# A hand-written instruction order: its first third and its identity products replaced

## The chip, the core and the metric

One core of a Trainium2 chip. The metric is the time of one launch in microseconds, the median of the runs on the device; lower is better. The kernel before has 238.1 us as the median of three runs (237.83 to 238.64).

## What is computed

An attention with blocks sorted by a Sinkhorn matrix, then a feed-forward network with a PReLU between its two products. Batch 4, 8 heads, 768 positions in 8 blocks of 96, head width 64; the network has 3072 tokens, width 512 and 2048 hidden units.

```python
for _ in range(5):                      # Sinkhorn: P is 4 x 8 x 8 x 8
    P = np.exp(P - np.max(P, axis=-1, keepdims=True))
    P = P / (np.sum(P, axis=-1, keepdims=True) + 1e-09)
    P = P / (np.sum(P, axis=-2, keepdims=True) + 1e-09)
k_sorted = np.einsum('bhij,bhjcd->bhicd', P, k_b)
v_sorted = np.einsum('bhij,bhjcd->bhicd', P, v_b)
scores = scale * np.matmul(q_b, k_sb.transpose(0, 1, 2, 4, 3))
attn = softmax(scores)                  # rows of one block of 96
out = np.matmul(attn, v_sb)
h = x @ w_in                            # x: attention output, heads side by side
y = (np.maximum(h, 0.0) + alpha * np.minimum(h, 0.0)) @ w_out
```

## The kernel before

**Work.** Attention is cut into 32 groups: group g is block g % 8 of batch g // 8, with all 8 heads. For each group there are: `s1`, the scores (8 products, L712 for batches 1 to 3, L715 for batch 0); the row maximum on VectorE (L721); the exp on ScalarE; `o`, the product with sorted v (L768); reciprocal and scaling on VectorE (L776, L779); and a turn of the result into xT, by TensorE and a copy in batches 0 and 1 (L794, L800) and by a transposing DMA later (L787). Batch 0 uses another way to the exp: the scores are made a second time, transposed, and the maximum is subtracted by products with the identity (L736 and L727, called `s2` here), so that one exp (L759) gives what `o` reads. In the other batches the exp (L748) is turned by a transposing DMA (L753).

**Preparation.** q, k and v are loaded by GpSimd's queue, which casts to bf16. For batch 0 `prep_q` turns q on TensorE (L600) and ScalarE copies the result out; for batches 1 to 3 a transposing DMA on SyncE's queue, `turn_q` (L409), does it. `prep_k` and `prep_v` (L629 and L669; L600 and L674 in batch 0) multiply k and v by a matrix that holds the Sinkhorn weights, 6 and 8 steps for each batch, each followed by a copy out of PSUM (0.6 to 0.7 us, L372) on ScalarE or VectorE. Before that, `conv_k` and `conv_v` (L616, L653, L658) spread the loaded k and v in SBUF, fp32 words copied on GpSimd or VectorE. The Sinkhorn rounds alternate between VectorE (L515 to L532) and one exp on ScalarE per round (L521). `spread0` and `spread` (L539, L557, L560) bring the result to all partitions; the matrix BDK is made on VectorE (L543).

**The network.** `ffn1(ga, gb, ft)` makes one tile of 128 hidden units for the tokens of groups ga to gb (4 products, L823), of 192 tokens for groups 0 to 3 and of 384 later; ScalarE takes the negative part (L833) and VectorE combines (L836). `ffn2(t)` makes 128 tokens of the result in four parts of 4 products (L863), then a copy (L372) and a store on SyncE's queue (L877). `w_in` and `w_out` come in four and two loads on GpSimd's queue (L908, L913).

**Order.** No scheduler runs when the kernel is built. Each operation is added to a graph with its reads and writes, and with a duration in nanoseconds; `arrange` (L158) then puts the operations on their engines in the order of the table `SEQ` (L36), whose numbers are the operations in the order in which they were added (a letter names the engine where there is a choice: p GpSimd, a ScalarE, d VectorE). Each engine, and each DMA queue, works strictly in that order. `emit` (L205) sets semaphore waits from the reads and writes. Neither reads the durations. `WARM` (L32) lists identity products: `89:14:y` puts 14 products of 128 x 512 with the identity before operation 89 on TensorE, into a PSUM bank whose content nobody reads (L808); four more are an operation of their own (L965).

Operations that the text speaks of: 44, 51, 58, 65, 72 the exps of the Sinkhorn rounds; 79 `spread0`; 81 to 92 `prep_q` and its copies; 93 to 105 `prep_k` of batch 0; 114 to 129 `prep_v` of batch 0; 149 and 158 `s1` of groups 0 and 1, 150 and 159 their maxima; 151 and 160 their `s2`; 134 and 135 the two loads of w_out; 273 to 276 `ffn2(0)`; 178 to 183 `turn_q` of batch 1; 402 and 403 the loads of v, 404 that of k for batch 2; 411 to 418 the loads of q for batch 2; 419 `s1` of group 8, 420 its maximum; 519 the `ffn1` tile at which the common order of TensorE begins.

## Time and profile before

| | |
|---|---|
| median of 3 runs | 238.1 us |
| span of the profiled execution, first to last instruction | 236.6 us |
| around the span (median less span) | 1.5 us |
| TensorE busy | 229.2 us (97%) |
| VectorE, ScalarE, GpSimd busy | 169.8, 151.6, 73.0 us |
| DMA moved | 31.36 MB |

The profile is of one execution, and its own time outside the span isn't recorded; the median less the span stands for it. Busy time of TensorE holds the identity products, and ends of products are modelled, so the distance from the start of one group of products to the start of the next is the better measure of what a group takes. In a timeline row stand start, length, engine, line, operation, tiles, and in brackets the idle time of the engine before it and what ended it. "PEld" is the weight load of TensorE. "DMA share" in the windows can be over 1, since packets overlap.

### The profile page before, as it was taken

Reading aid. Unit: us, or ns where it says so; the run is one execution under the profiler, and the core shown is the slowest. Engines: PE = TensorE matmul, PEld = TensorE weight load, DVE = VectorE, ACT = ScalarE, POOL = GpSimd, SP = SyncE. Lnnn points to the kernel's source line nnn. Section 1 sums busy time; section 2 is a strip of 40 time slices with the busy share of each in tenths; the row PEclk is TensorE's granted clock in tenths of the full one; section 3 lists DMA queues with packets and bytes.
Section 4 is the critical chain, followed back from the end, with each engine's and each line's share of the span. In section 5 each row is a group of like instructions: output and inputs, shape, how many; then the busy total and the mean of one; then the engine's idle time right before and its main releaser. Section 6 shows DMA issues by size and latency. Waiting matters only on the chain.

```text
span 236.6 us, 6266 instructions
## 1 busy us (share of the span) xinstructions
PE 229.2 (97%) x2532; PEld 142.2 (60%) x2532; DVE 169.8 (72%) x354; ACT 151.6 (64%) x423; POOL 73.0 (31%) x139
## 2 busy tenths in 40 slices
PE   7998998999999999999999999999999999999995
PEld 3446676687666666556566665655555555555543
DVE  4748796989899997868887667676766587744350
ACT  4475265587887988886678786756864646453332
POOL 7958812915659620338590020000000000000000
PEclk9999999999999999999999999999999999999999
DMA  5999999999989999899998796542642323400033
GB/s 96 212 213 168 211 217 202 179 209 158 191 88 167 152 120 173 119 210 166 165 111 114 188 164 135 98 90 52 125 92 82 97 50 79 140 0 1 0 133 135
DMA packets 71453, 31.36 MB, mean 133 GB/s; under 512 B 64504, under 2 KB 65280, under 8 KB 71424
## 3 DMA queue, kind: packets, MB, share of 16 engines
q0 software_dynamic: 22896, 13.63, 42.0%
q1 hardware_dynamic: 48528, 17.33, 37.8%
q8 instruction: 20, 0.33, 0.5%
q14 instruction: 9, 0.07, 0.1%
HBM read 27.28 MB, written 6.29 MB: 142 GB/s over the span
## 4 chain that ended last, share of the span: by engine, by line
PE 76%; DMA 17%; POOL 6%; issue 1%; ACT 0%; POOLq 0%
PE psH L823 31%; PE psYP L863 28%; DMA w_out_bf<-in_moe_w_out_dram 10%; PE psS L863 3%; PE psS L712 3%; DMA VST<-in_v_dram 3%; PE psO L768 3%; PE psYP L669 2%; DMA ET<-Esb 2%; PE psYP L629 1%; DMA QTz<-QN 1%; POOL w_in_bf L908 1%; PE psO L863 1%; PE psS L727 1%; POOL VDz L456 1%; PE psO L794 1%
## 5 line engine op out<-in xcount | busy, mean ns | idle before, releaser
L836 DVE SCALAR_TENSOR_TENSOR hT<-t,omaT,psH 128x384 bf16<-128x384 f32 (+1 forms) x139 | 77.4, 571 | 36.6 <-ACT t L833 35.1
L823 PE MATMUL psH<-xT,w_in_bf 128*128 128x384 bf16 (+1 forms) x556 | 96.9, 311 | 0.0
L833 ACT ACTIVATE t<-psH 128x384 f32<-128x384 f32 (+1 forms) x139 | 63.1, 461 | 50.3 <-PE psH L823 49.2
L863 PE MATMUL psYP<-w_out_bf,hT 128*128 128x512 bf16 x336 | 83.2, 379 | 1.3 <-DMA w_out_bf<-in_moe_w_out_dram 1.3
L823 PEld LDWEIGHTS psH<-xT,w_in_bf 128*128 128x128 bf16 x556 | 49.5, 98 | 28.9 <-DVE hT L836 1.6
L863 PEld LDWEIGHTS psYP<-w_out_bf,hT 128*128 128x128 bf16 x336 | 30.8, 98 | 30.1 <-DMA w_out_bf<-in_moe_w_out_dram 1.8
L748 ACT ACTIVATE Esb<-psS,nf 96x96 bf16<-96x96 f32 x192 | 46.1, 345 | 2.0 <-DVE nf L721 2.0
L721 DVE TENSOR_REDUCE nf<-psS 96x8 f32<-96x768 f32 x24 | 22.8, 951 | 6.4 <-PE psS L712 6.0
L658 POOL COPY VDz<-VST 64x192 f32<-64x192 f32 x39 | 20.4, 524 | 20.3 <-DMA VST<-in_v_dram 16.6
L779 DVE TENSOR_TENSOR xq<-psO,rec 96x512 bf16<-96x512 f32 x31 | 21.2, 683 | 0.5
L401 POOL DMA_DIRECT2D QN<-in_q_dram x24 | 19.8, 833 | 3.3 <-DMA QTz<-QN 2.7
L616 POOL COPY KSz<-KS 64x256 f32<-64x256 f32 x28 | 11.1, 397 | 31.6 <-PE psYP L629 19.8
L712 PEld LDWEIGHTS psS<-KT,QTz 128*96 128x96 bf16 x192 | 12.1, 124 | 3.3 <-DMA QTz<-QN 0.2
L768 PEld LDWEIGHTS psO<-VS,ET 112*128 112x128 bf16 x248 | 11.1, 98 | 3.6 <-ACT ET L759 0.2
L808 PE MATMUL psYP<-identb 128*128 128x512 bf16 x40 | 12.8, 453 | 0.4 <-ACT identb L372 0.4
L372 ACT ACTIVATE VS<-psYP 112x512 bf16<-112x512 f32 x15 | 10.3, 687 | 4.2 <-PE psYP L669 2.2
L768 PE MATMUL psO<-VS,ET 112*128 112x65 bf16 x248 | 12.7, 194 | 0.0
L712 PE MATMUL psS<-KT,QTz 128*96 128x96 bf16 x192 | 12.6, 208 | 0.0
L372 ACT ACTIVATE KT<-psYP 128x512 bf16<-128x512 f32 x15 | 9.0, 599 | 2.8 <-PE psYP L629 1.8
L669 PEld LDWEIGHTS psYP<-BDV,VDz 128*128 128x128 bf16 x192 | 8.2, 98 | 2.7 <-POOL VDz L658 0.4
L372 ACT ACTIVATE outstg<-psYP 128x512 f32<-128x512 f32 x13 | 7.7, 604 | 3.2 <-PE psYP L863 3.2
L669 PE MATMUL psYP<-BDV,VDz 128*128 128x64 bf16 x192 | 9.5, 193 | 0.2 <-POOL VDz L658 0.2
(137 smaller groups left out, 198.8 us busy)
## 6 DMA issues: line engine op xcount, KB each, us to landing
out_dram<-outstg SPq DMA_DIRECT2D x23, 256.0 KB, 2.5
KS<-in_k_dram POOLq DMA_DIRECT2D x3, 768.0 KB, 13.3
QN<-in_q_dram POOLq DMA_DIRECT2D x24, 96.0 KB, 4.4
w_in_bf<-in_moe_w_in_dram POOLq DMA_DIRECT2D x4, 512.0 KB, 17.3
w_out_bf<-in_moe_w_out_dram POOLq DMA_DIRECT2D x2, 1024.0 KB, 23.9
VST<-in_v_dram POOLq DMA_DIRECT2D x4, 384.0 KB, 17.6
hT<-in_q_dram POOLq DMA_DIRECT2D x1, 768.0 KB, 7.6
VST<-in_v_dram POOLq DMA_DIRECT2D x1, 768.0 KB, 11.1
```

The source lines that it names most:

```text
L372: return e.activation(o, i, ACTF.Copy) if e is nc.scalar else e.tensor_copy(o, i)
L658: G.add(SHIFT, lambda e, o2=o2, i2=i2: e.tensor_copy(o2, i2), {"dve": 424, "pool": 525}, r=vst, w=[("VDz", u % VSL, th)], prio=prio)
L669: inst = e.matmul(AP(t, off + dd * 64, [[row, 128], [1, 64]]), AP(VDz, (u % VSL * 4 + dd // 2) * 256 + dd % 2, [[VSL * 1024, 128], [2, 128]]),
L712: inst = e.matmul(o, AP(QTz[n], hp * 3072 + h4 * 768 + i * 96, [[6144, 128], [1, 96]]), AP(KT[n], (h4 * 8 + i) * bk, [[ld, 128], [64, 2], ...
L721: G.add(DVE, lambda e: e.tensor_reduce(AP(nx, 0, [[8, 96], [4, 2], [1, 4]]), AP(psX, 0, [[1024, 96], [512, 2], [96, 4], [1, 96]]), AxisLis ...
L748: inst = e.activation(AP(Esb[me], p * 128, [[1024, 96], [64, 2], [1, 48]]), AP(psX, (p // 4) * 512 + (p % 4) * 96, [[1024, 96], [48, 2], [ ...
L768: inst = e.matmul(AP(psZ, hp * 512 + h4 * 68, [[1024, 128], [1, 65]]), AP(ET[me] if far else ET[m], pos(h4, hp) * 96, [[800, nk], [1, 128] ...
L779: G.add(DVE, lambda e: e.tensor_tensor(out=AP(xq[me], 0, [[512, 96], [256, 2], [64, 4], [1, 64]]), in0=AP(psZ, 0, [[1024, 96], [512, 2], [ ...
L823: inst = e.matmul(AP(pt, poff, [[1024, 128], [1, n]]), AP(w_in_bf, kt * DFF + ft // 2 * 256 + ft % 2, [[KT_TILES * DFF, 128], [2, 128]]), ...
L833: G.add(ACT, lambda e: e.activation(AP(t1[tb], 0, [[384, 128], [1, n]]), AP(pt, poff, [[1024, 128], [1, n]]), ACTF.Relu, scale=-1.0), t_ac ...
L836: G.add(DVE, lambda e: e.scalar_tensor_tensor(out=AP(hT, ft * RING + tok % RING, [[FT_TILES * RING, 128], [1, n]]), in0=AP(t1[tb], 0, [[38 ...
L863: inst = e.matmul(AP(bank[0], bank[1], [[1024, 128], [1, n]]), AP(hT, ft * RING + tok % RING, [[FT_TILES * RING, 128], [1, 128]]), AP(w_ou ...
```

## The change

`SEQ` and `WARM` are replaced, and the durations given to `G.add`. The operations, their reads and writes, the buffers and the loads are the same 1227. TensorE's order differs in its first 145 operations and is the same in the last 254; SyncE's order differs in the first 14 of 85; on GpSimd the last 42 operations, on ScalarE the last 156 and on VectorE the last 189 are in the same order, and what stands ahead of them differs. 47 operations change engine (copies out of PSUM between ScalarE and VectorE; `conv_k` and `conv_v` between GpSimd and VectorE; on balance GpSimd has nine operations fewer, VectorE seven more, ScalarE two more). The identity products of the list go from 43 to 30. Some places, counted from 1 on the engine named:

| operation | before | after |
|---|---|---|
| loads of k and v, batch 0 (5, 6), GpSimd | 6, 8 | 3, 4 |
| first load of w_in (130), load of k, batch 1 (138), GpSimd | 13, 10 | 6, 12 |
| exp of Sinkhorn round 5 (72), ScalarE | 10 | 7 |
| maxima of groups 1 and 0 (159, 150), VectorE | 52, 56 | 50, 51 |
| `s2` of group 2 (186), TensorE | 37 | 35 |
| `ffn2(0)`, first part (273), TensorE | 49 | 61 |
| `s1` of group 8 (419), TensorE | 100 | 106 |
| loads of v for batch 2 (403, 402), GpSimd | 49, 62 | 61, 65 |

```diff
@@ -30,56 +30,57 @@
 WARM = """
-89:14:y 79:8:y 93:2:y 104:2:y 158:6:y 118:1:y 128:4:y 162:1:y 153:3:h 205:1:y 207:1:y
+83:15:y 79:2:y 100:2:y 158:7:y 160:1:y 136:1:y 156:2:i
 """
 
 SEQ = """
-0 7 11 2 3 1 4 8 9 22 42 28 14 43 44 45 46 19 47 18 5 48 49 50 15 51 39 52 53 6 54 55 25 56 138 57 58 23 29 59 12p
-60 61 130 62 63 64 31 65 32 66 37 13 67 68 89 69 83 81 70 84 71 87 131 10 91 88 85 132 72 40 73 90 74 133 75 86 76
-41 77 82 134 78 79 92 26 80 147 93 148 102 94d 103a 104 95 105a 100 98 96a 99a 97d 109d 106p 35 111d 112d 108p 34
-16 101a 36 38 33 107p 158 149 114 115d 146 110p 118 250p 159 116 248p 119a 120 113p 121d 124 30 117d 160 135 125a
-249p 254p 24 136 161 122 137 144 150 126 127a 143 123d 145 128 151 129d 253p 247d 20 17 152 162 21 163 164 141 153
-177 154 140 155 165 156 142 166d 184 157a 167 185 196 193 168 186 169 194 197 195 199 198 187 202 170 27 203 205
-200 204 188 201 214 206 220 215 217 189 218 207 221 219 222 226 216 229 190 227 223 230 273 228 224 171 208 231 225
-235 191 236 238 192a 237 232 239 261 251 262 209 313p 233 252a 240 210 263 347p 211 139 255 241 270 234 212 403 264
-256a 213d 291 404 301d 271 242 175 259 292 258p 274 260a 257p 272 265 352p 267 243 266 279 244 311p 293 280 268
-300p 281 282 269 312p 294 245 174 304d 285 310p 246d 275 286 351p 283 287 284 338 348p 302 339 295 305p 303a 314
-288 296 315 306 289 316 340 307a 290 176 297 320 341 317 276 318 178 321 319 298 322 379 299a 308 380 323 179 309a
-342 326 324 343 349 344 327 381 350a 325 328 345 353 382 346d 329 354d 332 330 383 333 331 357 277a 334 180 335
-572p 384 361 385 336 402 373 362 337 360p 358a 183 363 419 359d 574p 386 364 420 391p 367 365 374 355p 368 366 421
...
+0 7 2 17 10 3 1 4 8 9 5 42 11 6 43 44 14 45 46 47 48 130 49 50 51 32 52 23 53 54 22 55 26 56 25 57 28 138 58 37
+40 16 59 33 13 60 61 62 63 64 65 24 83 66 19 81 67 21 87 68 91 131 69 85 70 89 71 132 72 39 73 74 29 133 82 75
+76 38 77 20 78 88 12p 79 92 134 80 86 35 100 84 147 93 102 94a 98 95 101a 99d 104 90 105d 96a 103a 97p 158 107d
+113p 149 106d 116 108d 110p 18 159 118 114 111p 119a 150 15 160 117a 115a 109d 124 34 112p 122 125a 120 123d 161
+136 121d 128 126 129d 151 127a 137 162 152 177 163 164 36 248p 153 165 148 154 184 155 166a 250p 185 135 156 167
+157a 146 186 168 169 143 170 196 187 193 247d 139 253d 199 194 205 200 195 144 197 188 201 202 198 249p 206 214
+142 217 215 254d 203 41 207 218 204 216 220 189 171 208 219 223 190 226 221 224 238 222 227 191 225 229 192a 228
+232 239 209 233 235 230 210 236 234 240 231 237 264 211 241 251 261 252d 258p 212 262 291 140 265 175 263 255
+273 266 256a 257p 292 145 259 270 213d 174 293 141 260d 271 272 242 301p 294 282 172 243 304d 267 244 279 312p
+268 338 351d 305p 245 269 274 313p 300d 246a 339 280 404 283 295 302 281 310p 340 303a 284 352p 296 297 288 348p
+341 285 298 347p 306 286 299d 289 379 287 311p 307a 342 290 314 380 308 315 317 309a 275 176 343 318 27 316 319
+349 320 344 276 321 350d 323 322 353 356d 324 326 354d 359p 381 355p 325 277d 357 31 382 329 178 358d 345 373
+330 327 360d 346a 328 179 331 383 388 384 332 390d 389a 395p 335 385 374 180 333 391p 336 334 30 337 392 403 361
...
@@ -375,16 +376,16 @@
...
-        op = G.add(PE, f, t_pe(*[(n, 128)] * 4), r=[("xT", g % 16) for g in range(ga, gb)] + [("w_in", ft // 8 * 2 + x) for x in range(2)],
+        op = G.add(PE, f, {192: 330, 384: 650}[n], r=[("xT", g % 16) for g in range(ga, gb)] + [("w_in", ft // 8 * 2 + x) for x in range(2)],
...
```

The other hunks change durations alone, as the last one shown does.

More of the change, by code (lines that the diff above doesn't have):

```diff
@@ L514, in dv @@
         def dv(fn, r, w):
-            G.add(DVE, fn, 210, r=r, w=w, prio=pr)
+            G.add(DVE, fn, 191 if w[0] in ("rs", "cs") and w == r else 255 if w == ["cs"] else 208, r=r, w=w, prio=pr)
         for it in range(5):
@@ L562, in f @@
             return inst
-        G.add(PE, f, 100 * rows, r=["Pb", "selk"] + [("xT", 1)] * late, w=PSP, prio=prio)
+        G.add(PE, f, 130 * n + 110, r=["Pb", "selk"] + [("xT", 1)] * late, w=PSP, prio=prio)
         for y, mk in ((0, "mkj"), (1, "mkjV"))[:1 + late]:
@@ L607, in prep_q @@
         t, off, row, keys = bank
-        G.add(PE, pairs(hT, 8192, u, identb, 0, 128, bank), 372, r=[("QS", 0), "identb"], w=keys, prio=prio)
+        G.add(PE, pairs(hT, 8192, u, identb, 0, 128, bank), 254, r=[("QS", 0), "identb"], w=keys, prio=prio)
         o = AP(QTz[0], 8 * u, [[6144, 128], [96, 32], [48, 2], [1, 8]])
         i = AP(t, off, [[row, 128], [2, 32], [1, 2], [64, 8]])
-        G.add(ACT, lambda e: copy(e, o, i), t_act(512), r=keys, w=[("Q0", u)], prio=prio)
+        G.add(ACT, lambda e: copy(e, o, i), 569, r=keys, w=[("Q0", u)], prio=prio)
     def conv_k(b, u, prio):
@@ L633, in prep_k @@
         if b:
-            G.add(PE, f, 250, r=[("KSz", u % 3, hp) for hp in range(2)] + [("BDM", b)], w=keys, prio=prio)
+            G.add(PE, f, 232, r=[("KSz", u % 3, hp) for hp in range(2)] + [("BDM", b)], w=keys, prio=prio)
         else:
-            G.add(PE, pairs(KS[n], 0, u, BDK, 0, 512, bank), 372, r=ks + [("BDK", 0)], w=keys, prio=prio)
+            G.add(PE, pairs(KS[n], 0, u, BDK, 0, 512, bank), 254, r=ks + [("BDK", 0)], w=keys, prio=prio)
         ld, bk = 4 * NB * BK0, BK0
@@ L678, in prep_v @@
         if b:
-            G.add(PE, f, 250, r=[("VDz", u % VSL, th) for th in range(2)] + [("BDV", b)], w=keys, prio=prio)
+            G.add(PE, f, 232, r=[("VDz", u % VSL, th) for th in range(2)] + [("BDV", b)], w=keys, prio=prio)
         else:
-            G.add(PE, f, 374, r=[("VD", u), "VD0", ("BDK", 0)], w=keys, prio=prio)
+            G.add(PE, f, 277, r=[("VD", u), "VD0", ("BDK", 0)], w=keys, prio=prio)
         o = AP(VS[n], 8 * u, [[64 * 65, 112], [65, 64], [1, 8]])
         i = AP(t, off, [[row, 112], [1, 64], [64, 8]])
-        G.add(EITHER, lambda e: copy(e, o, i), {"act": 685, "dve": 690}, r=keys + [("VS1", n)], w=[("VS", n, u)],
+        G.add(EITHER, lambda e: copy(e, o, i), {"act": 687, "dve": 690}, r=keys + [("VS1", n)], w=[("VS", n, u)],
               prio=prio)
@@ L890, in burst @@
         return inst
[L891 removed]
+    G.add(PE, burst, 1240, r=["bz"], w=["psSw", "psS0", "psS1"], prio=-120)
     load_q(0, -98)
@@ L964, in bass_sinkhorn_attn__then__act_prelu_kernel @@
             spread([1, 2, 3], 1)
-            G.add(PE, lambda e: warm(e, 4, (psH, 0)), 300, r=["identb"], w=[("psH", 0, 0), ("psH", 0, 1)], prio=1)
+            G.add(PE, lambda e: warm(e, 4, (psH, 0)), 864, r=["identb"], w=[("psH", 0, 0), ("psH", 0, 1)], prio=1)
         if b + 1 < B:
```

180 lines of the change are left out of this document (90 added, 90 removed).

## The prediction

> **What bounds the kernel now.** I read the page first, then the busy time by stages, then the timeline of each engine through the first 80 us, then the rows of single lines. The page says that TensorE is the bound:
>
> ```profile
> span 236.6 us, 6266 instructions
> PE 229.2 (97%) x2532; PEld 142.2 (60%) x2532; DVE 169.8 (72%) x354; ACT 151.6 (64%) x423; POOL 73.0 (31%) x139
> DMA  5999999999989999899998796542642323400033
> ```
>
> But 97% holds the identity products that only fill waits, and matmul ends are modelled. The windows, cut at the first FFN1 product, at the stop for w_out, at the first score product of batch 1 (s1 of group 8) and where the two orders of TensorE become the same, tell more (busy us, granted clock, DMA share, GB/s):
>
> ```profile
> 0.00:8.90 8.90, 6.86 (x144) 2.98 (x144) 4.96 (x28) 3.24 (x8) 7.33 (x20) 1.00 0.71 133
> 8.90:28.70 19.80, 18.49 (x450) 12.38 (x450) 13.26 (x40) 10.78 (x21) 15.73 (x28) 1.00 1.05 199
> 28.70:36.40 7.70, 6.40 (x96) 5.20 (x91) 7.00 (x19) 4.37 (x12) 1.82 (x3) 1.00 1.13 217
> 36.40:56.90 20.50, 20.46 (x325) 16.17 (x326) 16.70 (x42) 14.12 (x34) 8.55 (x18) 1.00 1.43 193
> 56.90:79.20 22.30, 22.30 (x262) 14.77 (x261) 21.12 (x40) 18.18 (x58) 16.95 (x31) 1.00 1.25 148
> 79.20:236.60 157.40, 154.72 (x1265) 90.66 (x1264) 106.75 (x190) 100.90 (x292) 22.63 (x43) 1.00 0.62 110
> ```
>
> The columns are TensorE, its weight loads, VectorE, ScalarE and GpSimd. After 79.2 us TensorE has no slack, and the change leaves its order from there on (254 of 399 products) as it is. So the question is one number: how much earlier does TensorE stand at that point, the FFN1 product at 79.17 us? Up to 28.7 us TensorE is busy with little: the identity products take part of it, at 0.38 us each by the row and about 0.2 us from start to start (two in a row cover 0.59).
>
> ```profile
> L808 PE MATMUL psYP<-identb x40: 379/380/631, 2.8 to 32.9; 128*128 128x512 bf16 x40
> L808 PE MATMUL psH<-identb x7: 377/378/380, 25.7 to 27.2; 128*128 128x512 bf16 x7
> ```
>
> The stage is a chain of latencies through VectorE and ScalarE. Later TensorE stops once for a DMA (w_out at 36.40), and s1 of group 8 at 56.88 starts as the transposed q arrives (its weight load waits 0.2 us for it).
>
> **The change, part by part.** Three things move: the order of the first 145 products on TensorE with what feeds them, the engine of 47 copies, and the identity products (43 to 30 in the list, 4 more are an operation of their own). The durations in the code only served the search and cost nothing. Thirteen fillers less are 13 x 0.2 = 2.7 us less TensorE time, all of it in waits, so I count them at nothing by themselves: they neither hold up the chain nor shorten it where nothing else is earlier.
>
> First stage. The first 8.9 us are fixed by the load of q, issued first in both. Then these rows, ScalarE, VectorE and TensorE:
>
> ```profile
> 9.66 0.60 ACT L372 ACTIVATE QTz<-psH 128x512 bf16<-128x512 f32 x1 [1.15 <-PE psH L600]
> 10.66 0.24 ACT L521 ACTIVATE P<-P 32x64 f32<-32x64 f32 x1
> 16.43 1.08 ACT L372 ACTIVATE KT<-psO 128x512 bf16<-128x512 f32 x2 [0.36 <-PE psO L600]
> 25.30 0.81 ACT L759 ACTIVATE ET<-psS 112x768 bf16<-112x768 f32 x1 [1.53 <-PE psS L727]
> 9.82 0.21 DVE L532 TENSOR_TENSOR P<-P,cs 32x64 f32<-32x64 f32 x1
> 16.60 0.34 DVE L653 COPY hT<-VST 128x192 f32<-128x192 f32 x1 [0.21 <-DMA VST<-in_v_dram]
> 19.30 0.94 DVE L721 TENSOR_REDUCE nm<-psH 96x8 bf16<-96x768 f32 x1
> 21.94 0.94 DVE L721 TENSOR_REDUCE nm<-psS 96x8 bf16<-96x768 f32 x1
> 28.43 0.95 DVE L721 TENSOR_REDUCE nm<-psS 96x8 bf16<-96x768 f32 x1 [0.28 <-PE psS L715]
> 25.39 0.42 PE L768 MATMUL psYP<-VS,ET 112*128 112x65 bf16 x8
> 30.26 0.50 PE L823 MATMUL psYP<-xT,w_in_bf 128*128 128x192 bf16 x4
> ```
>
> The last exp of the Sinkhorn rounds stood ready at 10.03 (9.82 + 0.21) and ran at 10.66, behind two copies of transposed q. The new order has the exp first; three mask reductions slipped into round three cost some 0.2 us of it; so the chain is 0.5 us earlier. The six q copies and most of the KT copies then run on ScalarE, ten at about 0.5 us after 10.4 and 1.1 us of small things, done near 16.5 (before: 16.43 + 1.08 = 17.5): the first scores start at 16.75, 1.0 us earlier. v lands at 16.6 as before. VectorE now takes three copies of v (0.34 to 0.53 each), and both row maxima at once: 18.0 and 18.9 in place of 19.30 and 21.94. That is the largest gain: the second maximum no longer stands behind copies of VS. From there, in sequence: subtracting products of group 1 at 19.0; five more prep_v, each held by a bank that a 0.7 us copy empties, to 22.0; exp of group 0 at 23.0 (before 25.30); output product of group 1 at 23.0 (25.39); maximum of group 2 at 25.45 (28.43); and the group {s2 of group 2, two FFN1 steps} ends at 27.85 where it ended at 30.26. **Lead 2.4 us**; its bounds are 1.0 (the lead of the scores alone) and 3.0 (that of the maximum of group 2).
>
> The stop for w_out. GpSimd issues w_out as ninth transfer in both orders, behind the same bytes (only the first quarter of w_in and batch 1's k change places ahead of it), so it lands near 36.4 again. The product that waited for it
>
> ```profile
> 36.40 1.04 PE L863 MATMUL psYP<-w_out_bf,hT 128*128 128x512 bf16 x4 [1.27 <-DMA w_out_bf<-in_moe_w_out_dram]
> ```
>
> is moved 12 places back (49th to 61st), behind 3 to 4 us of other products. The 1.27 us go. What is late next? Three things can end last before s1 of group 8, which stands six products later in the new order:
>
> TensorE itself. From 30.26 to 56.88 are 26.6 us; less the stop and two fillers (1.27 + 0.4), plus the six products that are now ahead (0.86 + 0.33 + 0.17 + three of 0.23, read as distances of starts below: 2.1), 27.0. From 27.85 that is 54.9.
>
> ```profile
> 56.02 1.03 PE L863 MATMUL psYP<-w_out_bf,hT 128*128 128x512 bf16 x4
> 56.88 0.52 PE L712 MATMUL psS<-KT,QTz 128*96 128x96 bf16 x8
> 57.24 0.34 PE L794 MATMUL psO<-identb,xq 96*128 96x96 bf16 x4
> 57.41 0.82 PE L823 MATMUL psH<-xT,w_in_bf 128*128 128x192 bf16 x8
> 58.94 0.40 PE L669 MATMUL psYP<-BDV,VDz 128*128 128x64 bf16 x8
> ```
>
> The transposed q. Its loads stand behind the same queue of loads as before, so the first transposition is issued near 50.95 again, and lands 3.1 to 7.3 us later:
>
> ```profile
> 50.95 11.79 SPq L409 DMA_TRANSPOSE QTz<-QN  x5
> DMA to landing us min/median/max: 3.1/4.6/7.3
> ```
>
> That is 54.1 to 58.3; before it was 56.7 (56.88 less the 0.2 us wait). One of the two v loads that shared the DMA with it is now issued later, so I take 56.0.
>
> VectorE. It was busy 7.00 + 16.70 = 23.7 of the 28.2 us between 28.7 and 56.9. The new order puts 16 more operations (20 in, 4 out) before the maximum of group 8: net three copies of k, four of v, five of KT or VS, one of the output, one FFN1 step, two small ones.
>
> ```profile
> L616 DVE COPY KSz<-KS x8: 275/291/507, 25.0 to 137.9; 64x256 f32<-64x256 f32 x8
> L658 DVE COPY VDz<-VST x9: 322/432/552, 57.0 to 123.1; 64x192 f32<-64x192 f32 x9
> L372 DVE CAST VS<-psYP 112x512 bf16<-112x512 f32 x7 | 4.8, 689 | 0.0
> L836 DVE SCALAR_TENSOR_TENSOR hT<-t,omaT,psH 128x192 bf16<-128x192 f32 x27 | 10.2, 405 | 1.3 <-ACT t L833 0.9
> ```
>
> 3 x 0.29 + 4 x 0.43 + 6 x 0.69 + 0.41 + 0.3 = 7.4, less 16 overlaps of 0.08 (0.94 us operations start 0.87 apart: 19.30, 20.17) = 6.2. So 29.9 of work, and from 25.45 no earlier than 55.4. Before, it also stood 4.5 us idle, about 2 of them with TensorE's stop; I take 1.7 of waits: 57.1. This ends last of the three, so s1 of group 8 starts near 57.0, as late as before, but with six products more behind it. This is where most of the lead is given back.
>
> From there before: 79.17 - 56.88 = 22.3; less the 2.1 us done ahead, 20.2: **77.2, or 2.0 us earlier**. In that stage VectorE's load falls by the same copies (from 21.12 busy), so it has room. Behind it the loads of v for batch 3 ended the chain once (0.25 us idle at TensorE); q for batch 2 is now loaded in one run without copies between, so they should not come later; I count nothing for it.
>
> Sum: 236.6 - 2.0 = 234.6 for the profiled execution. Its span stands 1.5 us under the median of 238.1; 1.5 us around the span are kept. **Forecast 236.2.**
>
> A rule that speaks against the change: before the maximum of group 8 VectorE has ten fp32 copies of k and v in place of three, beside GpSimd's own. The rows above have such copies at 0.28 to 0.55 us, and
>
> ```profile
> 16.71 1.97 POOL L653 COPY hT<-VST 128x192 f32<-128x192 f32 x3 [2.49 <-DMA VST<-in_v_dram]
> 19.41 0.54 POOL L653 COPY hT<-VST 128x192 f32<-128x192 f32 x1
> ```
>
> three on GpSimd took 1.97 while VectorE copied, where 3 x 0.54 = 1.6 would do. The Trainium skill, "SBUF — State Buffer", section "SBUF: two separate sides", says that VectorE in a two-port mode and GpSimd share a port pair under an exclusive lock, so that one waits out the other; it adds that GpSimd then cannot write descriptors. The spread of the rows agrees. At the upper ends of the rows (0.51 and 0.55) the ten would add some 1.7 us; they count in the next rival.
>
> **The rivals.**
> - VectorE becomes the bound (slower). With the idle share of before, 4.5 of 23.7, its 29.9 become 35.6, and the maximum of group 8 starts at 61.0. s1 stands just ahead of it: 60.7 + 20.2 = 80.9, so 1.7 us later: 239.8. It decides from 59.0 on. For it: 6.2 us more work in a stage that was 84% busy, and the longer copies. Against: its one long wait, about 2 us, came from TensorE's stop. Chance 0.15.
> - The lead is given back to within 0.7 us, at VectorE or at the transposed q (58.3 at its slowest: 78.5, so 0.7 earlier): 237.4 to 238.8. Chance 0.21.
> - No wall holds and TensorE runs through: 54.9 + 20.2 = 75.1, 4.1 us earlier: 234.0. It needs the q transposition within 4 us, and VectorE without waits. Chance 0.08.
> - The clock falls. The granted clock is 1.00 in every window above, with the fillers in. The longest idle stretch that I find without the thirteen is about 1 us, near 11.5. At half clock the six prep_k and eight prep_v (some 0.25 us each) and two subtracting groups (0.8 us) between 11 and 23 us would take 5 us more; with 3.2 of it on the chain the lead of 2.4 becomes a loss of 0.8, VectorE's bound moves from 57.1 to 60.3, and the end to 239.3. Chance 0.03.
> The Trainium skill, "TensorE: Matmul & The Clock Gate", section "What's actually happening", puts the fall to half clock at an idle window of about 3.4 us; by that it does not come here.
>
> **How the numbers follow.** The forecast has 0.51, and 0.02 is left for what I don't see (counted as same). About 0.3%, or 0.7 us, is what this measurement can tell from none. Faster: 0.51 + 0.08 + 0.03 of the second rival, 0.62. Same: 0.16 of the second and the 0.02, 0.18. Slower: 0.15 + 0.03 + 0.02 of the second, 0.20. The range, 234.0 to 239.0, reaches from the run-through to half of the slower rival.
>
> **What would show it.** In the changed profile: exp of Sinkhorn round five near 10.1; the two first maxima near 18 and 18.9; FFN1 by 27.2 and no idle TensorE for w_out; VectorE over 90% busy from 28 to 57; s1 of group 8 at 56 to 58; the FFN1 product of 79.17 at 77.2; granted clock 1.00. It is wrong if that product is not earlier, if VectorE shows over 3 us idle before group 8, or if it is earlier and the end is not.

## The result, and the profile after

The changed kernel is slower by 0.6%. It takes 240.39 us in the median of 7 runs (239.03 to 246.42) beside 237.83 us (237.63 to 238.64) for the kernel before; the ratio is 1.0057, with a 95% interval of 1.0030 to 1.0085. The forecast was 236.2 us. The ratio leaves out runs more than 1.5% above a kernel's fastest; three of the seven are of that sort (243.11, 244.47 and 246.42 us), and the last part of the experiments is about them, as they turn out to be this order's own. The profiled execution took 239.03 us; its page begins

```profile
span 237.3 us, 6235 instructions
PE 228.2 (96%) x2519; PEld 141.8 (60%) x2519; DVE 171.4 (72%) x361; ACT 151.6 (64%) x425; POOL 69.7 (29%) x130
PEclk9999799999999999999999999999999999999999
```

The fifth slice of the granted clock (24 to 30 us) is below full speed, which it was nowhere before. The windows, cut at the same points as before (TensorE, its weight loads, VectorE, ScalarE, GpSimd, then granted clock, DMA share and GB/s):

```profile
8.90:28.70 19.80, 16.35 (x425) 11.67 (x425) 11.46 (x31) 11.19 (x23) 13.67 (x24) 0.91 1.05 201
28.70:36.40 7.70, 7.39 (x110) 5.65 (x110) 7.10 (x21) 4.39 (x12) 1.16 (x2) 1.00 1.12 215
36.40:56.90 20.50, 20.34 (x324) 15.83 (x322) 19.90 (x52) 11.86 (x29) 9.66 (x19) 1.00 1.40 189
56.90:80.40 23.50, 23.22 (x260) 15.03 (x258) 20.41 (x42) 20.83 (x68) 16.04 (x29) 1.00 1.08 146
80.40:237.30 156.90, 154.41 (x1269) 90.63 (x1264) 106.92 (x190) 100.53 (x289) 21.83 (x41) 1.00 0.63 110
```

The damage shows in the first of them: a clock of 0.91, and TensorE busy 2.1 us less than before. The stop for w_out is gone from the second (6.40 busy before), VectorE is 97% busy in the third, and the last is 0.5 us shorter than before. TensorE's timeline has the place:

```profile
16.96 0.38 PE L716 MATMUL psH<-KT,QTz 64*96 64x96 bf16 x8
18.67 0.41 PE L737 MATMUL psH<-QTz,KT 64*112 64x96 bf16 x8
19.83 0.62 PE L675 MATMUL psO<-BDK,hT 128*64 128x64 bf16 x24
22.57 0.32 PE L675 MATMUL psO<-BDK,hT 128*64 128x64 bf16 x8 [2.12 <-issue]
25.65 0.64 PE L769 MATMUL psYP<-VS,ET 112*128 112x65 bf16 x8
26.10 1.53 PE L809 MATMUL psH<-identb 128*128 128x512 bf16 x4
31.20 0.49 PE L824 MATMUL psYP<-xT,w_in_bf 128*128 128x192 bf16 x4
59.22 0.54 PE L713 MATMUL psS<-KT,QTz 128*96 128x96 bf16 x8
80.35 1.46 PE L824 MATMUL psH<-xT,w_in_bf 128*128 128x384 bf16 x8
```

Up to 20.3 us the forecast holds: scores at 16.96, s2 of group 1 at 18.67 (20.53 before). Then TensorE stands for 2.12 us in the middle of the sixteen products of one step of prep_v, called prep_v u3 here. (The row of 24 products holds the step ahead of it and its first eight, the next row its last eight.) No semaphore is named: "issue" is a wait for nothing that the profile shows. Behind it four identity products take 1.53 us, where four in a row took 1.03 before; the granted clock is low there (0.50 from 24 to 26 us and 0.72 from 26 to 28, in rows shown below).

To compare kernels with different orders I use one number, **TensorE's lag** at a time t: t less the fixed lengths of the kernel's own products that TensorE has done by then (FFN1 0.33 or 0.65 us, FFN2 0.86, s1 0.21 or 0.36, s2 0.78, output product 0.24, each prep near 0.25, and so on, the same list for all kernels; identity products count nothing). Its rise is time that TensorE gave to waits, fillers and a low clock. The lengths are estimates from rows, so a difference of 0.2 or 0.3 us in it says little. From the traces:

| kernel | 20 | 23 | 26 | 31 | 40 | 57 | 80 | 112 us |
|---|---|---|---|---|---|---|---|---|
| before | 13.9 | 15.0 | 16.7 | 17.5 | 20.1 | 21.3 | 21.4 | 22.3 |
| after | 13.0 | 15.6 | 16.7 | 18.3 | 20.0 | 21.5 | 22.6 | 22.9 |

The new order is 0.9 us ahead at 20, 0.6 behind at 23, 0.8 behind at 31, level at 40 (the w_out stop is in before's 20.1) and 1.2 behind at 80 us.

### The profile page after: what moved, and what is told of

Same layout as the page of the kernel before. It is cut to its first block, busy times and chain, and to the rows that moved or that the text cites. A ratio compares the mean times of both kernels' runs of the same rounds, so it can differ in the third digit from the quotient of the medians.

```text
span 237.3 us, 6235 instructions
## 1 busy us (share of the span) xinstructions
PE 228.2 (96%) x2519; PEld 141.8 (60%) x2519; DVE 171.4 (72%) x361; ACT 151.6 (64%) x425; POOL 69.7 (29%) x130
## 4 chain that ended last, share of the span: by engine, by line
PE 80%; DVE 14%; ACT 2%; issue 2%; DMA 1%
PE psH L824 31%; PE psYP L864 28%; DVE hT L837 4%; PE psS L864 3%; PE psS L713 3%; PE psO L769 3%; DVE nm L722 2%; PE psYP L670 2%; PE psYP L630 1%; PE psYP L809 1%; DVE VDz L659 1%; DVE nf L722 1%; PE psO L864 1%; DVE xq L780 1%; PE psS L728 1%
## 5 line engine op out<-in xcount | busy, mean ns | idle before, releaser
L659 POOL COPY VDz<-VST 64x192 f32<-64x192 f32 x33 | 17.6, 533 | 22.6 <-DMA VST<-in_v_dram 10.7
L780 DVE TENSOR_TENSOR xq<-psO,rec 96x512 bf16<-96x512 f32 x31 | 21.1, 682 | 0.5
L617 POOL COPY KSz<-KS 64x256 f32<-64x256 f32 x25 | 10.0, 400 | 36.7 <-PE psYP L630 29.7
L373 ACT ACTIVATE VS<-psYP 112x512 bf16<-112x512 f32 x14 | 9.7, 691 | 3.0 <-PE psYP L675 2.1
L373 ACT ACTIVATE outstg<-psYP 128x512 f32<-128x512 f32 x14 | 8.4, 606 | 3.2 <-PE psYP L864 3.2
L809 PE MATMUL psYP<-identb 128*128 128x512 bf16 x28 | 9.1, 462 | 1.0 <-issue 0.6
L373 DVE CAST VS<-psYP 112x512 bf16<-112x512 f32 x12 | 8.2, 687 | 0.9 <-PE psYP L670 0.8
## 6 DMA issues: line engine op xcount, KB each, us to landing
w_in_bf<-in_moe_w_in_dram POOLq DMA_DIRECT2D x4, 512.0 KB, 17.4
```

What stands on the lines that cost most here:

```text
L373: return e.activation(o, i, ACTF.Copy) if e is nc.scalar else e.tensor_copy(o, i)
L659: G.add(SHIFT, lambda e, o2=o2, i2=i2: e.tensor_copy(o2, i2), {"dve": 340, "pool": 518}, r=vst, w=[("VDz", u % VSL, th)], prio=prio)
L780: G.add(DVE, lambda e: e.tensor_tensor(out=AP(xq[me], 0, [[512, 96], [256, 2], [64, 4], [1, 64]]), in0=AP(psZ, 0, [[1024, 96], [512, 2], [ ...
```

## The experiments

My first theory was **instruction supply**. The page's DMA queues name 20 instruction packets:

```profile
q8 instruction: 20, 0.33, 0.5%
```

In the trace they are of 16,384 bytes each. TensorE has 2519 products and as many weight loads; 5038 instructions in 20 packets are 252 each, so I take a packet to be a block of 256 instructions of 64 bytes. Counting TensorE's instructions from the start (weight loads, products and the few others), the pauses without a wait end when 705 and 961 have run (15.78 and 22.57 us), 256 apart. In the trace packets start at 13.48, 20.10 and 27.79 us, the first two 2.3 and 2.5 us ahead of the ends of the two pauses. If a block is asked for when the one before it is begun, the packet of 20.10 was due at 15.78, and it stood over 4 us behind the loads (DMA share 1.05). No row shows the asking itself; but in the first 30 us of every trace kept here a packet starts behind each such count and ahead of the next, and each pause at one ends 2.2 to 2.6 us behind the start of a packet. The Trainium skill, "Runtime: NRT & Kernel Launch", section "Terms", says that an engine's instruction memory is refilled in 16 KiB blocks; the packets agree. The rival: the pause is prep_v u3's own (its data, its PSUM bank).

**after_wide, before_wide.** The burst of zeros at the very start is made of 6 wide products in place of 130 narrow ones:

```diff
-BURST = 130
+BURST = 6
...
-            inst = e.matmul(AP(psS, r * 1024 + 384, [[1024, 32], [1, 32]]), bz[r:r + 32, :], bz[r:r + 32, :])
+            inst = e.matmul(AP(psS, r * 1024, [[1024, 32], [1, 512]]), bz[r:r + 32, :], AP(bz, r * 32, [[32, 32], [0, 16], [1, 32]]))
```

> The changed kernel with the 130 narrow matmuls of the opening burst (32 columns each, 1.24 us in all) replaced by 6 of 512 columns on the same zeros: 248 fewer TensorE instructions ahead of everything else, no other edit. Theory (instruction supply): TensorE gets its instructions in blocks of 256, a block is asked for only when the one before is begun, and while the loads fill the DMA it takes 5.5 to 6.8 us to arrive; every block's edge then moves to 248 instructions later in the work, and the pause without a wait in the transpositions of prep_v u3 (2.2 us at 20.3 us) shrinks to 1.1 us or goes, the granted clock stays above 0.9 in 22 to 28 us, the group {s2 of g2, two FFN1 steps} ends at 28.0 to 29.5 us rather than 31.2, and the time is 236.0 to 238.5 us. Rival (the pause belongs to that operation: its data, its PSUM bank): the pause stays in prep_v u3 with 2 us or more, the group ends at 31 us, the time is within 0.3% of the changed kernel's 239.0 to 240.4 us.

> The kernel before with the same edit of the burst (130 narrow matmuls to 6 of 512 columns). Theory (instruction supply): its two pauses without a wait, 0.59 us at 16.1 and about 0.6 us at 22.3, go or move to 248 instructions later; it gains at most that, 0 to 1 us: 236.8 to 238.0 us. Rival: both pauses stay at their operations and nothing changes, 237.6 to 238.6 us.

after_wide has a ratio to before of 1.0065 (1.0038 to 1.0092), as without the edit. The pause stayed, 2.40 us until 22.70. But the expectation had a slip: edges repeat every 256, so 248 instructions fewer put the next edge only 8 instructions earlier in the work, and the block is asked for as late as before. The page shows one packet less:

```profile
q8 instruction: 19, 0.31, 0.5%
```

before_wide (1.0014, 0.9996 to 1.0032) was more telling. The same 8 instructions put the pause of the kernel before into another operation, the subtracting products (L727), and it was longer than any that it had:

```profile
23.30 0.25 PE L727 MATMUL psH<-identb,nm 96*112 96x96 bf16 x1 [1.21 <-issue]
```

So the kernel before takes such a pause, and one of 1.15 us at 16.7, without a loss that shows.

**after_b64.** The test with a shift that is no multiple of 256:

```diff
-BURST = 130
+BURST = 64
```

> The changed kernel with 64 narrow matmuls in the opening burst in place of 130: 132 TensorE instructions fewer ahead of the rest, so every edge of a 256-instruction block lies 132 instructions later in the work. (With 248 fewer the edge had only moved by 8, back to the same operation, as 248 is nearly a whole block.) Theory (instruction supply): the pause of 2.2 us leaves prep_v u3; a pause of 0.5 to 2.5 us stands in another operation, 132 instructions on, with s2 of group 2 or the identity products around it (24 to 26 us), and one near 18.5 to 19.5 us in the copies' products before s2 of group 1. The time is within 1.5 us of the changed kernel's, on either side, by whether the clock falls behind the new pause. Rival (the pause is that operation's own): it stays in prep_v u3, 2 us or more.

It measured 242.18 us, 1.0161 (1.0127 to 1.0194). prep_v u3 has no pause. Three other places have one, when 449, 705 and 961 of TensorE's instructions have run, 256 apart:

```profile
14.87 0.53 PE L601 MATMUL psYP<-BDK,KS 64*64 64x64 bf16 x12 [1.30 <-issue]
21.54 0.25 PE L675 MATMUL psO<-BDK,hT 128*64 128x64 bf16 x4 [1.12 <-issue]
28.56 0.29 PE L769 MATMUL psYP<-VS,ET 112*128 112x65 bf16 x2 [1.86 <-issue]
```

The rival is out: where the pause stands is set by the instruction count. The times of the three were not those that I gave, and the loss (1.0161 beside 1.0057, or 2.5 us) is beyond the 1.5 that I allowed. The granted clock is 0.50 behind two of them, from 15 to 18 us and from 28.6 to 31.8.

**after_gap.** Is it the loads that hold the block up? Seven loads go out later:

```diff
-... 46 47 48 130 49 50 ... 57 28 138 58 ... 91 131 69 ... 71 132 72 ... 29 133 82 ... 92 134 80 ... 84 147 93 ...
+... 34 112p 130 138 131 132 133 134 147 122 125a ...
```

> The changed kernel with seven load issues (the four parts of w_in, k of batch 1, the first part of w_out, the first part of v of batch 1) moved back on GpSimd's queue, behind its four copies of v: they go out from about 18.5 us on, so that the DMA falls idle when v of batch 0 has landed at 16.6 us, until 19 us or later. Nothing else moves. Theory (instruction supply: the block asked for at 15.8 us stands behind the loads until 20.1 us): the instruction packet comes at 16 to 17.5 us in place of 20.1, the pause of 2.2 us in prep_v u3 shrinks to under 0.6 us, and the transpositions up to the exp of group 0 come some 2 us earlier. FFN1 then waits for w_in, so the whole time is no test: 239 to 243 us. Rival (the pause has nothing to do with the loads' traffic): 2 us or more at the same operation.

The packet came at 17.24 in place of 20.10. The DMA moved nothing else from 15.5 us on, as v of batch 0 had landed by then (share and GB/s are the last two columns; the third row is the pause's place):

```profile
16.00:18.00 2.00, 2.00 (x68) 1.43 (x66) 2.00 (x6) 0.26 (x2) 1.82 (x4) 1.00 0.03 8
18.00:20.00 2.00, 2.00 (x59) 1.62 (x58) 1.53 (x4) 1.96 (x4) 1.88 (x4) 1.00 0.00 0
20.00:22.00 2.00, 2.00 (x56) 1.55 (x51) 1.75 (x3) 1.25 (x3) 2.00 (x4) 1.00 0.55 54
22.00:24.00 2.00, 2.00 (x30) 1.40 (x29) 1.11 (x4) 1.34 (x3) 2.00 (x4) 1.00 1.03 138
```

The changed kernel's own windows there are

```profile
20.00:22.00 2.00, 0.45 (x24) 0.34 (x19) 0.69 (x1) 1.35 (x2) 0.02 (x1) 1.00 1.01 202
22.00:24.00 2.00, 1.43 (x37) 1.14 (x37) 0.70 (x1) 0.00 (x0) 0.71 (x2) 0.93 1.09 205
24.00:26.00 2.00, 2.00 (x39) 1.84 (x34) 0.77 (x2) 0.80 (x2) 2.00 (x4) 0.50 1.12 199
26.00:28.00 2.00, 2.00 (x24) 1.08 (x21) 0.97 (x3) 0.80 (x2) 2.00 (x4) 0.72 1.07 187
```

In after_gap there is no pause and no fall of the clock here, and the chain is there sooner than forecast:

```profile
22.57 0.41 PE L768 MATMUL psYP<-VS,ET 112*128 112x65 bf16 x8
26.31 0.61 PE L727 MATMUL psS<-identb,nm 96*112 96x96 bf16 x8
```

The output product that stood at 25.39 before, 25.65 after and 23.0 in the forecast starts at 22.57. The lag at 26 us is 14.6, against 16.7 before: without the pause the lead is 2.1 us, and in the changed kernel it is gone at that time. The kernel before was not run with such a gap; its own pauses at the same two counts (0.51 and 0.52 us) would shrink too, so up to 1 us of the 2.1 may belong to the gap and not to the order. (FFN1 then waits 5.8 us for w_in, and the whole takes 243.74 us, 1.0240, a little over what I gave: it is no version to keep.)

The clock's part is harder to read. At half clock, from the rows above, are 0.28 + 2.0 + 1.12 = 3.4 us, which take 0.007 off the mean clock of the span. The runs of the changed order (after, after_again, after_v3, after_v3_again) below 242 us sort by just such steps: mean granted clock 1.00: 237.78 and 238.50 us; 0.993: 15 runs, median 239.44; 0.986: 11 runs, median 240.65. The kernel before has 60 of its 103 runs at 0.999 or more (median 238.0), 38 near 0.993 (238.3) and five lower. So one such stretch goes with 0.9 to 1.7 us in the new order and 0.3 in the old, and the two runs of the new order without one are no slower than before. They are no faster either, so the forecast of 236.2 was not missed for the clock alone. And a fall goes with a pause, so these times don't tell what the clock costs by itself.

**hb_ta, ha_tb.** Which part of the order loses? The two orders are spliced at operation 167 (30 us): hb_ta is before's head with after's rest, ha_tb the other way round:

```diff
-83:15:y 79:2:y 100:2:y 158:7:y 160:1:y 136:1:y 156:2:i
+89:14:y 79:8:y 93:2:y 104:2:y 158:6:y 118:1:y 128:4:y 162:1:y 153:3:h
...
-... 155 166a 250p 185 135 156 167 157a 146 186 168 ...
+... 165 156 142 166d 184 157a 167 185 186 168 ...
```

> The order (and fillers) of the kernel before up to operation 167, about 30 us, and of the changed kernel behind it. Theory (the loss lies ahead of 31 us, in the pause and the low clock behind it): TensorE stands at 30.3 us where the kernel before does, and the time is that of the kernel before or up to 1 us less: 236.8 to 238.2 us. Rival (the new order behind operation 167 is itself slower, by VectorE at 97% busy from 36 to 57 us and new waits to 80 us): 238.6 to 240.0 us.

> The order (and fillers) of the changed kernel up to operation 167, and of the kernel before behind it. Theory (the loss lies ahead of 31 us): the pause of 2.2 us and the clock of 0.5 stay, group {s2 of g2, two FFN1 steps} ends at 31.2 us, time 238.6 to 240.2 us. Rival (the loss lies in the new order behind it): 237.4 to 238.4 us.

My theory, that the loss lies ahead of 31 us, failed here. ha_tb has the pause (2.19 us until 22.75) and the low clock (0.50 from 23 to 29.5 us), and it equals before: 238.27 us, 0.9994 (0.9969 to 1.0018). hb_ta is worse than both: five of six runs took 243.9 to 249.1 us.

| kernel | 20 | 26 | 31 | 40 | 57 | 80 | 112 us |
|---|---|---|---|---|---|---|---|
| ha_tb | 13.1 | 16.9 | 19.6 | 20.8 | 22.1 | 22.4 | 22.7 |
| hb_ta | 13.5 | 16.4 | 17.7 | 19.3 | 21.0 | 22.0 | 27.2 |
| after_again | 13.0 | 16.9 | 19.3 | 20.8 | 22.5 | 23.5 | 29.0 |

ha_tb is 2.1 us behind before at 31 us and 0.8 at 57: the old order behind makes up for what the head loses. hb_ta is 0.8 ahead of before at 40 and 0.6 behind at 80. So what the new head loses does not reach the end where the old order follows; the loss at the end comes with the new order behind operation 167, as far as a splice can tell. And something near 108 us costs hb_ta 4 us, which the profiled execution of after doesn't have.

**The middle: before_273, ha419_tb, after_letters, after_dve_small, after_act_small.** In before_273 the product that waits for w_out goes ten places back, and nothing else moves:

```diff
-... 227 223 230 273 228 224 171 208 231 225 ...
+... 211 139 255 273 241 270 234 212 403 264
```

> The kernel before with one product moved: the FFN2 product that waits 1.27 us for w_out at 36.4 us goes 10 places back on TensorE, as the changed kernel has it nearly. One step of the prediction alone (the stop goes). If the lead lasts, 236.5 to 237.2 us (0.3 to 0.6% faster than before). If the lead is given back to VectorE or to the transposed q before s1 of group 8 (three walls at 55 to 57 us), the stop goes, s1 of group 8 stays at 56.5 to 57 us and the time is within 0.3% of before.

The time is 238.16 us, 1.0008 (0.9990 to 1.0026): no change. The lag is 19.2 at 40 (0.9 better than before), 21.1 at 57 (0.2 better). The next stop is for the second half of w_out:

```profile
45.61 0.81 PE L863 MATMUL psYP<-w_out_bf,hT 128*128 128x512 bf16 x3 [0.78 <-DMA w_out_bf<-in_moe_w_out_dram]
```

ha419_tb splices at operation 419 (s1 of group 8): after's order up to it, before's behind.

```diff
-... 396 365 363 419 573p 397a 366 367 394d 402 370 ...
+... 396 365 363 419 402 183 574p 420 367 368 366 ...
```

> The changed kernel's order (and fillers) up to operation 419, the first scores of group 8 at 59 us, and the order of the kernel before behind it. Theory (a third of the loss is made by the new order between 57 and 80 us, where TensorE waits 1.05 us in the changed kernel's profile and 0.14 in that of before): the FFN1 product at 80.35 us comes 0.6 to 0.9 us earlier, time 238.2 to 239.2 us, and no run above 242 us. Rival (these waits are the backlog of VectorE, 97% busy from 36 to 57 us, and come whatever the order behind): the product stays at 80 us or later, 239.0 to 240.4 us.

It took 240.41 us, 1.0106 (1.0080 to 1.0132). In its profiled execution TensorE came late to the edge: it had stood 2.00 us for VectorE until 12.88 us, and the clock was 0.50 behind that, from 14 to 17 us. The packet started at 19.81, so the pause at 22.23 us was only 0.40 us. The clock stayed at 1.00 from 22 to 30 us, and the lag at 57 us was 20.3, 1.0 better than before. Then TensorE's products waited 1.04 and 0.27 us for VectorE and ScalarE near 60 us, and the lag at 80 us was 22.3. There is no gain: the rival has it, though a splice may bring waits of its own.

> The changed kernel with 35 copies between 31 and 75 us (k, v, KT, VS, x and output copies, operations 246 to 480) on the engines that they have in the kernel before; the order of every engine else and the fillers are the changed kernel's. Theory (VectorE, 97% busy from 36.4 to 56.9 us, is what makes TensorE wait there and, by its backlog, up to 80 us): VectorE's share falls to 80 to 90%, TensorE's waits from 57 to 80 us fall from 1.05 us to 0.2 to 0.5, and the time by 0.5 to 1.2 us: 238.0 to 239.0 us. Rival (the waits come from the order on TensorE, not from the engine of the copies): 239.0 to 240.4 us, or longer where the copies are now late on the other engine.

```diff
-... 252d ... 260d ... 300d ... 299d ... 350d ... 358d ... 389a ... 393d ... 397a ...
+... 252a ... 260a ... 300p ... 299a ... 350a ... 358a ... 389d ... 393a ... 397d ...
```

It took 244.02 us, 1.0251 (1.0231 to 1.0271). VectorE's share fell to 84% (17.73 of 21 us from 36 to 57), and TensorE lost 3.5 us between 57 and 80 (19.49 of 23 busy). The letters belong to the order, so the run says nothing on VectorE as the bound. The next two leave work out, and so don't compute the whole result.

```diff
-            in0=AP(psZ, 0, [[1024, 96], [512, 2], [68, 4], [1, 64]]),
+            in0=AP(psZ, 0, [[1024, 96], [512, 2], [68, 4], [1, 8 if 4 <= g < 8 else 64]]),
...
-                AP(psX, 0, [[1024, nk], [512, 2], [1, 384]]),
+                AP(psX, 0, [[1024, nk], [512, 2], [1, 48 if 4 <= g < 8 else 384]]),
```

(The first for after_dve_small, the second for after_act_small; the other operands are cut alike.)

> The changed kernel with work left out on VectorE: of the four normalising multiplications of groups 4 to 7 (0.67 us each, at 43.8, 47.1, 51.0 and 56.6 us) only 8 of 64 columns are done, some 0.45 us less each, 1.8 us in all. Theory (VectorE's load binds from 36 us on and its backlog lasts to 80 us): TensorE reaches the FFN1 product of 80.35 us 0.7 to 1.5 us earlier (1.8 us is the most) and the time falls as much, to 238.0 to 239.0 us. Rival (VectorE is only busy beside TensorE; the waits come from the order): 0.4 us or less.

> The control: the changed kernel with work left out on ScalarE, the four exps of groups 4 to 7 (0.81 us each) on 96 of 768 columns, some 0.55 us less each, 2.2 us in all, in the same chain of the groups. Theory (VectorE binds, not ScalarE nor the length of the groups' chain): the time stays within 0.3% of the changed kernel's, or gains 0.4 us at most. Rival (the chain of the groups or ScalarE binds): 0.7 us or more earlier at the FFN1 product of 80.35 us, and more than without VectorE's work.

The ratios to before are 1.0061 (1.0024 to 1.0098) without VectorE's work and 1.0091 (1.0054 to 1.0129) without ScalarE's. From 31 to 80 us the lag rises by 4.1 us without VectorE's work, 4.3 without ScalarE's, 4.3 in after and 4.1 in after_v3_again, whose edit acts later. So 1.8 us less work on VectorE gains no more than the 0.2 us by which two such profiles differ anyway; its 97% lies beside TensorE. (In both profiles the long pause came one edge earlier, 1.79 and 2.08 us until 17.2 and 17.4, so their first 31 us are not those of after's.) What holds TensorE between 40 and 80 us I could not settle.

**The long runs: after_again, after_v3, after_v3_again, hb_ta_2, hb_ta_v3.** The four loads of v for batch 3 wait for one tile of batch 2's transposed q. The edit lets them go four tiles sooner by number, one or two us in time:

```diff
-                r=[("QTzt", 0, 5)] * (b == 3), w=[("VST", b % 2)] * (x == 0) + [("VST", b % 2, x)],
+                r=[("QTzt", 0, 1)] * (b == 3), w=[("VST", b % 2)] * (x == 0) + [("VST", b % 2, x)],
```

> The changed kernel with one dependence eased: the four loads of v for batch 3 wait for the transposition of tile 1 of batch 2's q and no longer for tile 5; they go out at about 92 us in place of 95.3. Nothing else. Theory (in a part of the runs of the new order these loads start too late, are still under way when the next output store and transpositions start near 101 us, and end 4 to 5 us later, which stops TensorE near 105 to 109 us by 2.5 to 4 us): runs above 242 us disappear, none of ten or more; the lower runs stay at 239.0 to 240.4 us. Rival (the long runs are a disturbance of the chip that comes to any order): one in six or more stays above 242 us.

> The kernel with the order of before up to operation 167 and the changed kernel's behind it (of which five runs of six were 243.9 to 249.1 us), with the loads of v for batch 3 freed as in the other experiment: they wait for tile 1 of batch 2's transposed q, not tile 5, and go out near 93 us, not 95.6. Theory (the long runs are those in which these loads are still under way when the next output store and transpositions start): one run in six or fewer is above 242 us, the median 238.3 to 239.5 us. Rival (the long runs have another cause): half or more stay above 242 us.

> The same kernel as hb_ta (order of before up to operation 167, the changed kernel's behind it), once more, on the same chip as its variant with the earlier loads. Theory: half or more of the runs above 242 us again, with TensorE stopped by 2 us or more near 105 to 109 us; rival (a disturbance of the chip in the first job): most runs at 238.5 to 239.5 us.

> The changed kernel itself, on the same chip as its variant with the earlier loads of v for batch 3. Theory: one run in five or more is above 242 us, and in a profile of such a run TensorE stands 2 us or more near 105 to 110 us behind these loads. Rival (the three long runs of seven were a disturbance): no run above 242 us.

> The changed kernel with the loads of v for batch 3 freed by tile 1 of batch 2's transposed q, not tile 5, once more, beside the unchanged one. Theory: no run above 242 us, so the median is lower than the unchanged one's if that has such runs, and the lower runs are equal. Rival: the same share of long runs in both.

Of the unchanged after, 3 of 7 and 8 of 14 (after_again, same code) were above 242 us, up to 248.3; with the edit 0 of 6 and 0 of 12, the highest 241.3. Variants without the edit have them too: after_wide 3 of 12, after_dve_small 4 of 12, after_act_small 5 of 11. Of hb_ta 5 of 6 and 4 of 4 (hb_ta_2); with the edit 2 of 6, none above 243. Of the kernel before 1 of 103. (The lower runs of after_again stand at 1.0036, 0.9993 to 1.0078; hb_ta_2 at 1.0298, 1.0264 to 1.0331, with TensorE stopped for 1.93 and 1.26 us near 110 us; hb_ta_v3 at 1.0131, 1.0098 to 1.0165, its median of 240.45 above what I gave.) In after's profiled execution GpSimd's rows are

```profile
95.30 2.12 POOL L436 DMA_DIRECT2D VST<-in_v_dram  x4 [5.74 <-DMA QTz<-QN]
102.38 1.67 POOL L659 COPY VDz<-VST 64x192 f32<-64x192 f32 x3 [4.96 <-DMA VST<-in_v_dram]
```

and in after_again's, a long run (span 246.5), GpSimd's and TensorE's are

```profile
96.93 2.12 POOL L436 DMA_DIRECT2D VST<-in_v_dram  x4 [6.62 <-DMA QTz<-QN]
110.36 1.65 POOL L659 COPY VDz<-VST 64x192 f32<-64x192 f32 x3 [11.32 <-DMA VST<-in_v_dram]
110.23 0.41 PE L769 MATMUL psO<-VS,ET 112*128 112x65 bf16 x8 [3.46 <-DMA ET<-Esb]
112.07 0.61 PE L670 MATMUL psYP<-BDV,VDz 128*128 128x64 bf16 x8 [1.43 <-POOL VDz L659]
```

Issued 1.6 us later, the same loads land 8 us later. In after's profile they are done (102.38) before SyncE's next two transpositions are issued, though two output stores (100.43) and the transposition ahead of them (98.87) overlap with them. In the long run the stores (102.15) and the two transpositions (103.61) start while the loads run. SyncE's rows of the two transpositions, after first, and then the windows of after and of after_again:

```profile
102.86 5.02 SPq L754 DMA_TRANSPOSE ET<-Esb  x2
103.61 7.57 SPq L754 DMA_TRANSPOSE ET<-Esb  x2
```

```profile
102.00:104.00 2.00, 2.00 (x23) 1.37 (x21) 1.06 (x3) 1.70 (x6) 1.50 (x3) 1.00 1.39 207
104.00:106.00 2.00, 2.00 (x15) 0.99 (x14) 1.76 (x3) 1.68 (x7) 0.05 (x1) 1.00 1.09 118
106.00:108.00 2.00, 2.00 (x30) 1.39 (x27) 1.18 (x3) 1.78 (x6) 1.44 (x3) 1.00 0.84 238
108.00:110.00 2.00, 2.00 (x25) 1.38 (x24) 1.91 (x5) 1.28 (x3) 1.46 (x4) 1.00 1.06 161
```

```profile
102.00:104.00 2.00, 1.95 (x16) 1.17 (x16) 1.49 (x3) 1.96 (x8) 0.00 (x0) 1.00 1.42 133
104.00:106.00 2.00, 2.00 (x19) 1.15 (x18) 1.35 (x2) 1.41 (x5) 0.00 (x0) 1.00 1.19 55
106.00:108.00 2.00, 0.77 (x4) 0.16 (x2) 0.74 (x2) 1.87 (x8) 0.00 (x0) 1.00 1.44 104
108.00:110.00 2.00, 0.00 (x0) 0.00 (x0) 0.00 (x0) 0.00 (x0) 0.00 (x0) 1.00 1.11 41
```

In the long run the DMA engines are full and move 41 to 133 GB/s, beside 118 to 238. So the loads stand at an edge: a run that is 0.9 us further behind at 80 us (lag 23.5 beside 22.6) falls over it, and its span is 9.2 us longer (246.5 beside 237.3). That these loads make the long runs is shown by the edit, which moves nothing else; that it is by overlapping with the transpositions is read from these two profiles. The kernel before issues them at 94.5 us, 0.8 us ahead of after. With the edit the loads are off the edge, but the kernel is still slower than before: after_v3 is at 1.0072 (1.0046 to 1.0097), after_v3_again at 1.0080 (1.0057 to 1.0103), and in the latter's profile a transposition stops TensorE for 1.20 us until 101.09. hb_ta_v3 is the plainest: it has before's head and the edit, and at 1.0131 it still loses.

**after_v3_gap1, mix_gap1.** A shorter gap in the loads, as an attempt at a version that beats both (mix_gap1 has before's order behind operation 167, with 273 moved):

```diff
-... 105d 96a 103a 97p 158 107d ... 34 112p 122 125a 120 ...
+... 105d 96a 103a 97p 130 158 107d ... 34 112p 138 131 132 133 134 147 122 125a 120 ...
```

> The changed kernel with the earlier loads of v for batch 3, and with a short gap in the loads: on GpSimd's queue the first part of w_in goes out behind the copy of KT (16.1 us), six further loads behind the copies of v (19.5 us), so that the DMA is free for about 1 us from 16.6 us on, when the instruction block that was asked for at 15.8 us waits. Theory (the fall of the clock behind the pause makes the 0.6%): pause in prep_v u3 under 0.8 us, granted clock of the run 1.00, time 237.2 to 238.4 us, 1.5 to 2.5 us less than without the gap (240.19 median). Rival (pause and clock are made good by later walls anyway): 239.3 to 240.5 us.

> The changed kernel's order up to operation 167 with the same gap in the loads, the order of the kernel before behind it, with its FFN2 product that waits for w_out ten places back. Theory (the lead of the new head is real once the pause is gone, and the old order behind it has no stop for w_out and no late loads of v): 236.2 to 237.6 us, faster than both kernels. Rival (any lead at 31 us is taken by the walls before 57 us, as it was with the moved product alone): 237.6 to 238.6 us, the same as before.

They took 241.78 us, 1.0149 (1.0104 to 1.0194), and 244.54 us, 1.0249 (1.0203 to 1.0295). In the first the pause is gone (lag 14.7 at 26 us, 2.0 ahead of before), but the first FFN1 product then stands 3.0 us until 30.2, in which the profile names no wait; the loads of w_in, issued up to 22.6 us, take 11.3 us in the median. The clock falls there (0.50 from 30 to 34 us). In the second the late block came one edge earlier (a pause of 1.97 us until 17.2). An FFN1 product then stood 2.05 us until 37.5, for which the profile names no wait, and w_out, later too, stopped TensorE for 1.60 us until 51.0. Both theories missed: among the loads that hold up the block are those of w_in, which are themselves needed before 30 us. No version that I ran beats both kernels.

## Why the prediction was wrong

The sum had three points in time. The FFN1 step that ends the first stage was said for 27.85 us and came at 31.20, 3.35 late. s1 of group 8 was said for 57.0 and came at 59.22, 2.2 late. The FFN1 product at the common order was said for 77.2 and came at 80.35, 3.15 late. Behind it the changed kernel took 0.5 us less than before. So in the profile the miss is made in the first stage, 1.1 us of it is made good in the second, and 0.9 lost again in the third.

- **Scores, maxima, s2 of group 1: right.** Exp of Sinkhorn round five at 10.12 (said 10.15), scores 16.96 (16.75), maxima 17.39 and 18.26 (18.0, 18.9), s2 of group 1 at 18.67 (19.0).
- **"five more prep_v, each held by a bank that a 0.7 us copy empties, to 22.0 ... Lead 2.4 us": the step that failed.** prep_v ran to 24.4, and that FFN1 step stood at 31.2: a loss of 0.9 us in place of the lead of 2.4. The working asked of each product which data and which bank it waits for; that TensorE's own instructions have to arrive was in no term. That wait was 2.12 us at the 961st instruction. The trace of before had the sign, pauses without a wait of 0.51 and 0.52 us at the same two counts, and I took them for part of the waits. Without the pause the lead is 2.1 us (after_gap), of which up to 1 us may be the gap's own.
- **A lead at 31 us was taken for a lead at the end; that failed too.** ha_tb is 2.1 us behind at 31 us and ends level with before (0.9994); hb_ta_v3 has before's head, no long runs above 243 us, and is 1.3% slower. So, as far as two splices can tell, the loss at the end is made with the new order behind operation 167, and a head without the pause might not have saved the forecast. What makes that loss stays open; VectorE's multiplications of groups 4 to 7 don't.
- **"The clock falls", chance 0.03: the clock did fall, but the match of the number is luck.** That rival gave a loss of 0.8 us in place of the lead and 239.3 us; measured are 0.8 us at 31 us and, at clock 0.993, 239.44. But it put the half clock between 11 and 23 us, behind thinner fillers. The clock fell behind the pause, near 24 us, and by the lag the new order had gone from 0.9 us ahead to 0.6 behind by 23 us, ahead of the fall. What the fall added after that was not separated. I weighed the rival by the idle stretch (1 us near 11.5) and by the Trainium skill, "TensorE: Matmul & The Clock Gate", section "What's actually happening", whose idle window is some 3.4 us. Here a pause of 2.1 us was enough, and in hb_ta_v3 one of 1.07 us until 21.96 (clock 0.54 from 22 to 24). The stretch at half clock, 3.4 us, is as long as that window.
- **"The 1.27 us go" (w_out): right and worth nothing.** In before_273 0.9 us at 40 us is 0.2 at 57; in ha419_tb 1.0 us still stands at 57 and is lost by 80. **The walls before s1 of group 8:** something takes such a lead back, but VectorE is not shown to be it, as without 1.8 us of its work nothing moved. That its stage came out nearly as long as I gave it (28.0 us from that FFN1 step to s1 of group 8, said 29.15) is luck.
- **"then 20.2 us" from s1 of group 8 to the common order: 21.1** (59.22 to 80.35), in a stage where I had counted room. The longest wait there is that of a weight load for VectorE, 0.67 us until 70.2; the longest of that stage before is 0.38 us.
- **The loads of v for batch 3, "I count nothing for it": wrong in half of the runs.** In a profile of such a run TensorE stands for 3.46 and 1.43 us near 110 us, and 11 of 21 runs were above 242 us. I said that the loads "should not come later"; they came 0.8 us later in the profile and 2.4 in a long run.
